# Early weights: two back steps alternate with the next weight's third and fourth front steps instead of its first and second

## The chip, the core and the metric

The kernel runs on one core of one Trainium2 chip. The metric is device time in microseconds; of several executions the median is given.

## The reference

Attention with exponential features, then two feed-forward layers, all in float32:

```python
def phi(x):                                  # for q and k, scaled
    proj = np.einsum('bhsd,md->bhsm', x, omega)
    sq = np.sum(x * x, axis=-1, keepdims=True) / 2.0
    h = proj - sq
    h = h - np.max(h, axis=-1, keepdims=True)
    return np.exp(h) / np.sqrt(m)
kv = np.einsum('bhsm,bhsd->bhmd', k_p, v)
num = np.einsum('bhsm,bhmd->bhsd', q_p, kv)
den = np.einsum('bhsm,bhm->bhs', q_p, z)[..., None] + 1e-06
...
xn = x / rms * rms_g
silu = g * (1.0 / (1.0 + np.exp(-g)))        # g = xn @ w_gate, val = xn @ w_val
x = (silu * val) @ w_out                     # first layer, d_ff 1536
g = h * np.cos(h)                            # h = x @ w_in
out = g @ w_out                              # second layer, d_ff 2048
```

There are 4 batches, 8 heads, 576 positions per batch (2304 tokens, 18 tiles of 128), head dimension 64, 128 features, model width 512.

## The kernel before

The work is one hand-written stream for each engine. First come 24 attention slots. Each slot projects one tile of 128 tokens (k tiles, with the first q tiles among them): TensorE multiplies by omega into two PSUM banks (`kp_ps` or `qp_ps`, L426), VectorE takes the maximum of each head (`kmx`, `qmx`, L435), ScalarE the exponential, head by head (`ke`, `qe`, eight a tile, L437). One slot later TensorE adds the k tile into its batch's sums (`kv_ps`, L587). When a batch is full, VectorE copies its two sums out (L598), which frees the banks for the next batch. A q tile goes through seven more steps, each in a later slot: transposes (`eT`, copied out half by VectorE, L454, and half by ScalarE, L452), the numerators (`num_ps`, L464) and quotients (L474 to L476), the square sum on ScalarE (`sq`, `ms`, L483), the root on GpSimd (L487, L488), the norm on VectorE (L492), a transpose (`xT_ps`, L502) and its split into high and low parts (`xhl`, L514, L516). Four banks are taken in turn by the projections and by `xT_ps`, so a projection waits until the exponentials of the tile that had the bank are done.

Then come FFN steps n = 0, 1, ...: products of a token block with a gate and a value weight (L831), their gating, and the output product (L884). The last q tiles go on beside them.

Beside all this the weights are made. They come as 64-bit floats: `raw` is a tile of pairs of 32-bit words, loaded by a DMA, and each weight must become a float32 (`f`) and then a pair of reduced-precision parts (`w`, high and low), so that three TensorE passes give nearly full precision. The class `Weights` holds this as generators whose steps are interleaved with the slots. The first 12 weights, c = 0 to 11, are the early ones (`self.fused`): they are made entirely in the attention slots and the first FFN steps. An early weight has six front steps (`front`, L186 to L211):

1. VectorE shifts `W` into `f` (L190);
2. only for a weight without signs in `W` (c = 2, 5, 8, 11): VectorE puts in the sign (L193);
3. VectorE masks the exponent into `raw` (L195);
4. ScalarE makes the next weight's `W` out of its `raw` (`exponent(c + 1)`, L182 or L184), so this waits for that raw weight's DMA;
5. VectorE multiplies the low word in (L204);
6. GpSimd adds both into `f` (L209).

and two back steps (`early_back`, `split`): ScalarE casts `f` to the high part of `w` (L214), behind which the load of raw weight c + 3 is issued on ScalarE's queue (L170); GpSimd subtracts for the low part (L217). `run` alternates the front steps of weight c with the back steps of weight c - 1, and every `tick` of a slot takes so many steps of `run`:

```python
for s in range(SLOTS):
    ...
    if s:
        wts.tick(5 if s < 6 else 1 if s < 14 else 4 if s + 1 < SLOTS else 0)
```

In the first FFN steps it is four steps for each half. Each engine takes its instructions strictly in the order in which the steps emit them; what stands behind a waiting instruction waits with it. Three raw tiles and three `f` tiles are held at a time, and one `W`.

Of the kernel before, what the change touches and what calls it, by code (L numbers as in the profile page):

```python
# [56 lines left out]
def attention_then_ffn(ctx: ExitStack, tc: tile.TileContext, qT, kT, v, omT, wc1, rms_g, wc2, out, B, H, S, D):  # L57
# [69 lines left out]
    class Weights:  # L127
# [186 lines left out]
        def run(self):  # L314

            self.exponent(0)
            yield
            for c in range(self.fused + 1):
                both = [self.front(c)] if c < self.fused else []
                if c > 0:  # L320
                    both.append(self.early_back(c - 1))
                while both:
                    for g in list(both):
                        if next(g, DONE) is DONE:
                            both.remove(g)
                        else:
                            yield
# [1102 lines left out]
```

## Time and profile before

| what | value |
|---|---|
| median of 3 runs | 966.22 us (966.13 to 969.75) |
| the profiled execution, its own time | 965.95 us |
| its span, from the first to the last instruction | 964.2 us |
| TensorE (PE) matmul / weight loads (PEld) | 951.0 us (99%) / 894.6 us (93%) |
| VectorE (DVE) / ScalarE (ACT) / GpSimd (POOL) | 710.2 us (74%) / 537.1 us (56%) / 415.5 us (43%) |
| ScalarE's casts of w (L214), 88 in all | 50.5 us, 580 ns each; 32.2 us of idle time before them |
| GpSimd's adds of f (L209), 68 in all | 94.3 us, 1387 ns each |
| granted clock of TensorE | 1.00 |

A profile's times count from the start of the span. The attention slots and the first FFN steps, in which the early weights are made, take about the first 130 us. Idle time is named with what ended it. Matmuls are pipelined, and their ends are modelled.

### The profile page before, as it was taken

Reading aid. Unit: us, or ns where it says so; the run is one execution under the profiler, and the core shown is the slowest. Engines: PE = TensorE matmul, PEld = TensorE weight load, DVE = VectorE, ACT = ScalarE, POOL = GpSimd, SP = SyncE. Lnnn points to the kernel's source line nnn. Section 1 sums busy time; section 2 is a strip of 40 time slices with the busy share of each in tenths; the row PEclk is TensorE's granted clock in tenths of the full one; section 3 lists DMA queues with packets and bytes.
Section 4 is the critical chain, followed back from the end, with each engine's and each line's share of the span. In section 5 each row is a group of like instructions: output and inputs, shape, how many; then the busy total and the mean of one; then the engine's idle time right before and its main releaser. Section 6 shows DMA issues by size and latency. Waiting matters only on the chain. (4 is left out here: it accounts for less than half of the span.)

```text
span 964.2 us, 16225 instructions
## 1 busy us (share of the span) xinstructions
PE 951.0 (99%) x5761; PEld 894.6 (93%) x5761; DVE 710.2 (74%) x1163; ACT 537.1 (56%) x1155; POOL 415.5 (43%) x377
## 2 busy tenths in 40 slices
PE   9999999999999999999999999999999999999998
PEld 8998999989999999999999998889889889889997
DVE  5786677778863686577685758996799777785766
ACT  7787776775543524355443545575655565464443
POOL 2133366657944867275764663320244220130000
PEclk9999999999999999999999999999999999999999
DMA  8565187778697898856989794967622768307554
GB/s 311 159 179 186 56 279 277 253 267 261 220 329 289 331 331 290 302 154 196 391 281 370 263 356 142 352 226 262 207 88 85 265 199 293 120 23 264 203 219 166
DMA packets 96082, 227.65 MB, mean 236 GB/s; under 512 B 9728, under 2 KB 45184, under 8 KB 96000
## 3 DMA queue, kind: packets, MB, share of 16 engines
q1 hardware_dynamic: 94704, 222.34, 67.0%
q10 hardware_dynamic: 1296, 4.26, 1.3%
q8 instruction: 46, 0.75, 0.3%
q14 instruction: 36, 0.29, 0.1%
HBM read 156.04 MB, written 70.52 MB: 235 GB/s over the span
## 5 line engine op out<-in xcount | busy, mean ns | idle before, releaser
L1251 PE MATMUL o_ps<-w,o 128*128 128x512 f32 x864 | 225.7, 393 | 0.7 <-DVE o L1054 0.7
L209 POOL TENSOR_TENSOR f<-f,raw 128x512 f32<-128x512 f32 x68 | 94.3, 1387 | 234.9 <-DVE raw L204 205.1
L1251 PEld LDWEIGHTS o_ps<-w,o 128*128 128x128 f32 x864 | 159.6, 188 | 25.0 <-DVE o L1054 1.1
L217 POOL TENSOR_TENSOR w<-b,w 128x512 fp32r<-128x512 f32 x88 | 115.3, 1316 | 136.7 <-ACT w L214 127.0
L831 PE MATMUL gv_ps<-xhl,w 128*128 128x384 f32 x576 | 108.0, 335 | 1.6 <-DVE gv L870 1.1
L831 PEld LDWEIGHTS gv_ps<-xhl,w 128*128 128x128 f32 x576 | 100.6, 188 | 2.2 <-DVE gv L870 1.4
L1150 PE MATMUL y<-t,w 128*128 128x384 f32 x576 | 102.1, 334 | 0.3 <-POOL w L217 0.3
L1150 PEld LDWEIGHTS y<-t,w 128*128 128x128 f32 x576 | 100.0, 188 | 0.6 <-POOL w L217 0.6
L1051 ACT CAST o<-turns 128x384 fp32r<-128x384 f32 x96 | 47.5, 513 | 95.0 <-DVE turns L1232 95.0
L1043 PE MATMUL Xh<-T,w 128*128 128x384 f32 x432 | 88.6, 340 | 1.7 <-ACT h L1196 1.7
L1043 PEld LDWEIGHTS Xh<-T,w 128*128 128x128 f32 x432 | 78.0, 188 | 9.2 <-ACT h L1196 4.0
L1043 PE MATMUL X<-T,w 128*128 128x384 f32 x432 | 80.9, 335 | 0.0
L1043 PEld LDWEIGHTS X<-T,w 128*128 128x128 f32 x432 | 75.3, 188 | 0.3 <-DVE r L1078 0.2
L214 ACT CAST w<-b 128x512 fp32r<-128x512 f32 x88 | 50.5, 580 | 32.2 <-DVE b L274 25.1
L1054 DVE TENSOR_TENSOR o<-turns,o 128x384 fp32r<-128x384 f32 x96 | 59.9, 640 | 8.2 <-ACT o L1051 8.1
L884 PE MATMUL y_ps<-t,w 128*128 128x384 f32 x288 | 60.7, 346 | 0.0
L1043 PE MATMUL Yh<-B,w 128*128 128x384 f32 x288 | 58.7, 338 | 0.0
L1199 DVE TENSOR_TENSOR h<-Yh,h 128x384 f32<-128x384 f32 x48 | 26.6, 553 | 42.4 <-PE Yh L1043 41.5
L1221 DVE SCALAR_TENSOR_TENSOR turns<-turns,r 128x768 f32<-128x768 int32 (+1 forms) x50 | 56.4, 1128 | 1.7
L1017 ACT ACTIVATE turns<-turns,half_pi 128x768 f32<-128x768 f32 (+1 forms) x50 | 45.7, 915 | 21.4 <-DVE turns L1221 21.3
L190 DVE TENSOR_SCALAR f<-W 128x512 int32<-128x512 int32 x68 | 44.8, 658 | 15.2 <-ACT W L182 6.5
L1043 PEld LDWEIGHTS Yh<-B,w 128*128 128x128 f32 x288 | 52.2, 188 | 3.8 <-ACT h L1196 0.2
(117 smaller groups left out, 1882.0 us busy)
## 6 DMA issues: line engine op xcount, KB each, us to landing
T<-T_dram SPq DMA_DIRECT2D x48, 768.0 KB, 7.0
raw<-wc SPq DMA_DIRECT2D x60, 512.0 KB, 4.9
B<-yh_dram SPq DMA_DIRECT2D x21, 768.0 KB, 5.4
kept<-f SPq DMA_DIRECT2D x56, 256.0 KB, 4.8
b<-kept SPq DMA_DIRECT2D x56, 256.0 KB, 4.9
B<-x_dram SPq DMA_DIRECT2D x15, 768.0 KB, 6.9
x_dram<-xhl SPq DMA_DIRECT2D x12, 768.0 KB, 5.8
s<-x_dram SPq DMA_DIRECT2D x24, 384.0 KB, 5.9
```

The lines of the kernel that those rows point to most:

```text
L209: nc.gpsimd.tensor_tensor(f32(f), f32(f), rest, op=ALU.add)
L214: nc.scalar.copy(t[:, 0, to], src)
L217: nc.gpsimd.tensor_tensor(t[:, 1, to], src, f32(t[:, 0, to]), op=ALU.subtract)
L831: nc.tensor.matmul(o, w[i], x[j], start=n == 0, stop=n == len(terms) - 1)
L884: nc.tensor.matmul(yacc[blk][e], w[:, i, e * P:(e + 1) * P], t[:, j], start=first and i + j == 0, stop=last and j == 1)
L1017: f(*args)
L1043: nc.tensor.matmul(o, w[:, i, c + kk * P:c + (kk + 1) * P], x[:, j, kk], start=begin and n == 0, stop=n == 5, skip_group_check=True)
L1051: nc.scalar.copy(t[:, 0], a)
L1054: engine.tensor_tensor(t[:, 1], a, f32(t[:, 0]), op=ALU.subtract)
L1150: nc.tensor.matmul(acc[e], w[:, i, e * P:(e + 1) * P], t[:, j], start=f == fs[0] and i + j == 0, stop=f == fs[-1] and j == 1)
L1221: nc.vector.scalar_tensor_tensor(r, a, -TWO_PI_LO, b, op0=ALU.mult, op1=ALU.add)
L1251: nc.tensor.matmul(oacc[blk][j], o[:, x, js], w[:, y], start=first and n == 0, stop=last and n == 2)
```

## The change

`run` lets the front generator of weight c take its first two steps alone; the back generator of weight c - 1 joins from the third round on (at once where there is no front left, for the last weight). A weight's eight steps were front 1, back 1, front 2, back 2, front 3, 4, 5, 6; they are front 1, 2, 3, back 1, front 4, back 2, front 5, 6.

```diff
             for c in range(self.fused + 1):
                 both = [self.front(c)] if c < self.fused else []
-                if c > 0:
-                    both.append(self.early_back(c - 1))
-                while both:
+                after = [self.early_back(c - 1)] if c > 0 else []
+                n = 0
+                while both or after:
+                    n += 1
+                    if n > 2 or not both:
+                        both += after
+                        after = []
                     for g in list(both):
                         if next(g, DONE) is DONE:
                             both.remove(g)
```

In the changed file the lines behind `run` are numbered four higher (L441 there is L437 here). The orders of TensorE, GpSimd and SP are the same but for these numbers. ScalarE's order moves in the early slots as follows. `ke3_0` are the exponentials of the first four heads of k tile 3; `w0`, `W3` and `raw3` belong to weights 0 and 3. Before:

```order
L437 ACTIVATE ke2_1_264<-kp_ps2_1_248,kmx2_1_265 128x128 x4
L214 CAST w0_283<-f0_239 128x512
L170 DMA raw3_285<-wc1 128x1024
L437 ACTIVATE ke3_0_302<-kp_ps3_0_292,kmx3_0_303 128x128 x4
L437 ACTIVATE ke3_1_309<-kp_ps3_1_293,kmx3_1_310 128x128 x4
L184 ACTIVATE W2_326<-raw2_201 128x512
L437 ACTIVATE ke4_0_343<-kp_ps4_0_333,kmx4_0_344 128x128 x4
L437 ACTIVATE ke4_1_350<-kp_ps4_1_334,kmx4_1_351 128x128 x4
L214 CAST w1_367<-f1_281 128x512
L170 DMA raw4_369<-wc1 128x1024
L437 ACTIVATE ke5_0_387<-kp_ps5_0_377,kmx5_0_388 128x128 x4
L437 ACTIVATE ke5_1_394<-kp_ps5_1_378,kmx5_1_395 128x128 x4
```

Changed, ScalarE at the same place:

```order
L441 ACTIVATE ke2_1_264<-kp_ps2_1_248,kmx2_1_265 128x128 x4
L441 ACTIVATE ke3_0_299<-kp_ps3_0_289,kmx3_0_300 128x128 x4
L441 ACTIVATE ke3_1_306<-kp_ps3_1_290,kmx3_1_307 128x128 x4
L214 CAST w0_321<-f0_239 128x512
L170 DMA raw3_323<-wc1 128x1024
L184 ACTIVATE W2_325<-raw2_201 128x512
L441 ACTIVATE ke4_0_343<-kp_ps4_0_333,kmx4_0_344 128x128 x4
L441 ACTIVATE ke4_1_350<-kp_ps4_1_334,kmx4_1_351 128x128 x4
L214 CAST w1_369<-f1_281 128x512
L170 DMA raw4_371<-wc1 128x1024
L182 ACTIVATE W3_373<-raw3_323 128x512
L441 ACTIVATE ke5_0_388<-kp_ps5_0_378,kmx5_0_389 128x128 x4
```

w0's cast and raw3's load moved behind the exponentials of k tile 3, and W3, which stood behind those of k tile 5, moved ahead of them. On VectorE the mask of raw1 (L195) moved ahead of the two maxima of k tile 3.

The second place is ScalarE around w4, in slots 15 and 16. Before, w4's cast stood between the exponentials of q tile 3 and k tile 12:

```order
L437 ACTIVATE qe3_1_862<-qp_ps3_1_846,qmx3_1_863 128x128 x4
L214 CAST w4_900<-f4_740 128x512
L170 DMA raw7_902<-wc1 128x1024
L437 ACTIVATE ke12_0_917<-kp_ps12_0_907,kmx12_0_918 128x128 x4
L437 ACTIVATE ke12_1_924<-kp_ps12_1_908,kmx12_1_925 128x128 x4
L514 CAST xhl0_0_774<-xT_ps1_931 128x2x128
L514 CAST xhl0_1_775<-xT_ps1_931 128x2x128
L483 ACTIVATE sq2_938,ms2_939<-x2_874 128x512
L452 COPY eT3_1_953<-eT_ps3_1_948 128x512
L182 ACTIVATE W6_958<-raw6_797 128x512
```

Changed, ScalarE at the same place:

```order
L441 ACTIVATE qe3_1_862<-qp_ps3_1_846,qmx3_1_863 128x128 x4
L441 ACTIVATE ke12_0_914<-kp_ps12_0_904,kmx12_0_915 128x128 x4
L441 ACTIVATE ke12_1_921<-kp_ps12_1_905,kmx12_1_922 128x128 x4
L518 CAST xhl0_0_774<-xT_ps1_928 128x2x128
L518 CAST xhl0_1_775<-xT_ps1_928 128x2x128
L487 ACTIVATE sq2_935,ms2_936<-x2_874 128x512
L456 COPY eT3_1_950<-eT_ps3_1_945 128x512
L214 CAST w4_953<-f4_740 128x512
L170 DMA raw7_955<-wc1 128x1024
L182 ACTIVATE W6_957<-raw6_836 128x512
```

w4's cast moved behind the square sum of q tile 2 (`ms2`) and the eT copy of q tile 3. GpSimd's order around it is the same before and after: w4's low part, then the two root steps of `ms2`, then the add of f5.

The third place is VectorE ahead of the maxima of k tile 17, the last k tile. Before:

```order
L204 SCALAR_TENSOR_TENSOR raw7_902<-raw7_902 128x512
L190 TENSOR_SCALAR f8_1220<-W8_1175 128x512
L435 TENSOR_REDUCE kmx17_0_1239<-kp_ps17_0_1228 128x4
L435 TENSOR_REDUCE kmx17_1_1246<-kp_ps17_1_1229 128x4
L193 SCALAR_TENSOR_TENSOR f8_1220<-W8_1175,f8_1220 128x512
L195 TENSOR_SCALAR raw8_1004<-f8_1220 128x512
```

Changed:

```order
L204 SCALAR_TENSOR_TENSOR raw7_955<-raw7_955 128x512
L190 TENSOR_SCALAR f8_1220<-W8_1174 128x512
L193 SCALAR_TENSOR_TENSOR f8_1220<-W8_1174,f8_1220 128x512
L439 TENSOR_REDUCE kmx17_0_1236<-kp_ps17_0_1225 128x4
L439 TENSOR_REDUCE kmx17_1_1243<-kp_ps17_1_1226 128x4
L195 TENSOR_SCALAR raw8_1062<-f8_1220 128x512
```

The sign step of f8 (L193) moved ahead of the two maxima. On ScalarE the cast of w7, which stood right ahead of the exponentials of k tile 17, moved behind them.

## Rows read from the trace of the kernel before

**Rows 1.** Windows, 10 to 90 us: us, busy time of each engine, clock, DMA.

```profile
10.00:90.00 80.00, 79.18 (x807) 72.95 (x804) 62.23 (x129) 66.74 (x220) 24.88 (x24) 1.00 0.65 211
```

**Rows 2.** Timeline of TensorE's weight loads: start, length, engine, line, what, count.

```profile
16.65 1.99 PEld L587 LDWEIGHTS kv_ps<-v,ke 128*128 128x128 f32 x16
...
29.39 1.86 PEld L587 LDWEIGHTS kv_ps<-v,ke 128*128 128x128 f32 x16
31.37 0.97 PEld L426 LDWEIGHTS qp_ps<-om,qraw 64*128 64x128 f32 x16
32.46 1.86 PEld L464 LDWEIGHTS num_ps<-kv,eT 128*128 128x128 f32 x16
```

**Rows 3.** Waits of ScalarE, 10 to 130 us: total us, times, longest.

```profile
ACT w L214 <- POOL f L209: 5.6, 6, 2.0
```

**Rows 4.** Timeline of ScalarE and, last two rows, VectorE in the early slots.

```profile
15.59 0.62 ACT L214 CAST w<-f 128x512 fp32r<-128x512 f32 x1 [0.50 <-POOL f L209]
15.65 0.37 ACTq L170 DMA_DIRECT2D raw<-wc  x1
16.12 2.18 ACT L437 ACTIVATE ke<-kp_ps,kmx 128x128 f32<-128x128 f32 x8
18.13 0.72 ACT L184 ACTIVATE W<-raw 128x512 f32<-128x512 f32 x1
...
21.22 2.29 ACT L437 ACTIVATE ke<-kp_ps,kmx 128x128 f32<-128x128 f32 x8
...
14.33 1.28 DVE L435 TENSOR_REDUCE kmx<-kp_ps 128x4 f32<-128x512 f32 x2
15.53 0.42 DVE L195 TENSOR_SCALAR raw<-f 128x512 int32<-128x512 int32 x1
```

**Rows 5.** Raw weights' landing: loads of ScalarE's queue (15 to 83 us), then all.

```profile
DMA to landing us min/median/max: 4.0/4.4/5.4
...
DMA to landing us min/median/max: 3.5/4.4/6.9
```

**Rows 6.** Timeline of TensorE's matmuls.

```profile
22.43 3.82 PE L587 MATMUL kv_ps<-v,ke 64*128 64x128 f32 x31
...
70.11 4.03 PE L587 MATMUL kv_ps<-v,ke 64*128 64x128 f32 x32
...
84.05 1.16 PE L426 MATMUL qp_ps<-om,qraw 64*128 64x128 f32 x14 [0.66 <-ACT ke L437]
```

**Rows 7.** Timeline of GpSimd, 59 to 66 us.

```profile
59.33 1.27 POOL L217 TENSOR_TENSOR w<-f,w 128x512 fp32r<-128x512 f32 x1 [0.73 <-ACT w L214]
62.71 0.19 POOL L487 TENSOR_SCALAR ms<-ms 128x1 f32<-128x1 f32 x1 [2.11 <-ACT sq L483]
62.98 0.55 POOL L488 TENSOR_TENSOR ms<-ms,minus_half 128x1 f32<-128x1 f32 x1
64.14 1.41 POOL L209 TENSOR_TENSOR f<-f,raw 128x512 f32<-128x512 f32 x1 [0.61 <-DVE raw L204]
```

**Rows 8.** Timeline of ScalarE, 62 to 85 us.

```profile
62.66 0.59 ACT L452 COPY eT<-eT_ps 128x512 f32<-128x512 f32 x1
...
82.33 0.62 ACT L214 CAST w<-f 128x512 fp32r<-128x512 f32 x1 [0.62 <-POOL f L209]
...
82.86 2.17 ACT L437 ACTIVATE ke<-kp_ps,kmx 128x128 f32<-128x128 f32 x8
```

**Rows 9.** Timeline of VectorE, 64 to 83 us.

```profile
64.32 1.77 DVE L492 SCALAR_TENSOR_TENSOR x<-x,ms,gain 128x512 f32<-128x512 f32 x1
...
68.69 0.75 DVE L598 COPY kv<-kv_ps 128x260 f32<-128x260 f32 x2
...
77.46 0.75 DVE L492 SCALAR_TENSOR_TENSOR x<-x,ms,gain 128x512 f32<-128x512 f32 x1
...
81.07 1.28 DVE L435 TENSOR_REDUCE kmx<-kp_ps 128x4 f32<-128x512 f32 x2
82.27 0.68 DVE L193 SCALAR_TENSOR_TENSOR f<-W,f 128x512 int32<-128x512 int32 x1
```

## The prediction

> **What bounds the kernel now.** I read the windows first. From 10 to 90 us, the stretch that holds most of the moved steps, TensorE shows 79.18 us of matmul in 80 us, all other engines less, at granted clock 1.00 [rows 1]. The reader should distrust that 79.18 a little, because a matmul that crawls counts as busy; so I read the weight loads next, whose share is 72.95 of 80. An undisturbed stretch prices their normal gaps: the loads that start at 29.39 and 31.37 are 1.86 and 0.97 us long, and the next group starts at 32.46, so 2.83 of 3.07 us are load and 7.8% is gap even where nobody waits [rows 2]. 7.8% of 80 is 6.25, the loads' idle time is 7.05: some 0.8 us of TensorE time is true waiting there. To it comes a group of loads that is stretched because ScalarE's exponentials feed it one head at a time: 1.99 us at 16.65 against 1.86 [rows 2], 0.13 us. So **all that this stage can give back is about 0.9 us**, 0.1% of the run, although ScalarE waits 5.6 us in six places for GpSimd in the very step that moves [rows 3]. Most of that wait lies beside TensorE's work.
>
> The profiled execution took 965.95 us (span 964.2); the median of the three runs is 966.22, 0.27 higher. I add the sum to either.
>
> **What the change does, part by part.** Work is neither added nor removed. Every early weight's two back steps (ScalarE's cast with the load of a raw weight behind it; GpSimd's low part) come two steps later, and the front steps between come one or two earlier. TensorE's, GpSimd's and SP's orders stay; ScalarE's and VectorE's change. After the attention stage the program is the same and TensorE stays full, so a shift of TensorE at 90 us should reach the end nearly whole.
>
> *The early slots.* Now the cast of w0 stands ahead of ke3's exponentials: it waits 0.50 us for f0's add and ke3 can start at 16.12 only [rows 4]. After, ke3 stands first, and VectorE's kmx3 gates it, which in turn has raw1's mask (0.42) put ahead of it: 14.33 + 0.42 + half of 1.28, some 15.4 [rows 4]. ke3 is 0.7 us earlier, and the loads at 16.65 are no longer fed one by one: **-0.13 us** (bounds 0 and -0.13).
>
> Against that stands raw3's load, a DMA on ScalarE's queue behind the cast: issued at 15.65 before, and some 17.7 after (ke3 from 15.4 takes 2.2). W3 moves the other way, ahead of ke5's exponentials. These loads take 4.0 to 5.4 us to land [rows 5], so raw3 is there at 21.7 to 23.1, while ScalarE, which began ke5 at 21.22 right behind w1's cast, is free for W3 near 21.6. W3 (0.72 by W2's row) and then ke5's 2.29 would end between 24.7 and 26.1, instead of 23.5 [rows 4]. TensorE uses ke5 in the second half of the accumulations that start at 22.43 and last 3.82, to 26.2 [rows 6]; at the undisturbed 1.98 for sixteen it starts there at 24.2 and needs the last exponential near 26.0. Cost **0**, bounds 0 and +0.3; were the load as slow as the slowest one of the start, 6.9 [rows 5], ke5 would end at 27.6 and TensorE lose 1.6. I take 0, as the median is 4.4.
>
> *The norm at 64 us.* This is where the change may hurt. GpSimd is in order: low part of w4, then the two ms2 steps, then f5's add. Now the low part is done at 60.6, ms2 runs from 62.71 to 63.53, and the add starts at 64.14 [rows 7]. After, w4's cast stands behind the eT copy that ends at 63.25, and lasts 0.62 [rows 8]: the low part runs from 63.9 to 65.2, ms2, stuck behind it, to 66.0 although its input was there at 62.7, and VectorE's norm, which ran at 64.32, starts 1.7 us later. The norm took 1.77 us with f5's add beside it and 0.75 alone [rows 9]; the add comes right behind ms2 again, so I take 1.77. From the norm VectorE is busy through kmx14 and the quotients to the copies of kv2 at 68.69 (0.75 for two) [rows 9], so these end near 70.8 and 71.1 instead of 69.1 and 69.4. TensorE's next accumulation needs the banks they clear; it started at 70.11 [rows 6] and would be due at 70.0 now. **+0.8 us**; bounds +0.1 (if the norm runs alone, 1.02 shorter) and +1.2 (if it needs both copies).
>
> The Trainium skill, "SBUF — State Buffer", section "SBUF: two separate sides", says that VectorE and GpSimd share one pair of ports as an exclusive lock: whoever starts first keeps it for its whole instruction, and a VectorE operation with two SBUF inputs waits it out. By that rule the norm would end 0.75 us after the add's 1.41, about 0.4 later than I took, the term would be +1.2 and the sum 0.4 higher. The row agrees in kind, not quite in size: 64.14 + 1.41 + 0.75 gives 66.30, and the norm ended at 66.09.
>
> *The wait at 84 us.* TensorE's one plain wait in the stage is 0.66 us on ScalarE before the row at 84.05 [rows 6]: qp5 needs a bank that the first four exponentials of ke17 clear, and these started at 82.86 because w7's cast (82.33, 0.62 us late on GpSimd) stood ahead [rows 8]. After, that cast is gone from there; but f8's sign step (0.68) now stands ahead of kmx17: 81.07 + 0.68 + half of 1.28 is 82.4 [rows 9], so ke17 can start 0.4 us earlier, if TensorE is on time. With TensorE 0.67 late by the terms above, what feeds kmx17 is as late, and ke17 starts at some 83.1: of the 0.67 us, 0.2 to 0.3 is left. **-0.4 us** (bounds 0 and -0.66).
>
> Costed at nothing: the casts of w8 to w10 move behind exponentials or copies in a stretch where ScalarE waits for VectorE and TensorE anyway; the casts and W steps that now stand together (w3 and W5, w5 and W7, w6 and W8) delay the exponentials behind them by up to one cast, 0.62 [rows 8], and TensorE uses these a group of matmuls later. If that cover were gone, each is worth its 0.62 once. The weights come two steps later and are first used when the FFN begins.
>
> **Sum**: -0.13 + 0 + 0.8 - 0.4 = +0.27 us: 966.2 for the profiled execution, **966.5** for the median. That is no change that a measurement of this kernel can tell (about 0.5%, 4.8 us).
>
> **Rivals.**
> 1. *Slower by the norm, with nothing given back.* The low part of w4 delays ms2, the norm and the copies at the upper bound of 1.2, and ke17 slides along so that the wait at 84 us stays: +1.2 - 0.13, 967.3. It decides once the norm starts over 0.6 us late, since the first copy ends 1.0 ahead of 70.11 and the rest is the bank's way to TensorE. For it: the fixed order and the busy VectorE. Against: 0.66 us of plain wait lies behind it.
> 2. *Slower by raw3.* The load lands in 6.9 us and W3 holds ke5: +1.6, and 0.1 of the rest, 967.9. Against: no load on ScalarE's queue took over 5.4.
> 3. *Faster.* The norm runs alone or beside nothing, and ke17 starts 0.4 us earlier: -0.13 - 0.4, 965.7, at most the 0.9 of the stage, 965.3. For it: the one long wait of the stage is touched.
> 4. *Much faster.* If every gap of the weight loads were headroom, 7.05 us could come back: 959.2. The gaps of the undisturbed stretch speak against it. The Trainium skill, "Perfetto Trace Analysis", section "Identifying the Most-Contended Engine", says to judge TensorE by its weight-load share rather than by matmul time; taken literally it reads the 72.95 this way.
> 5. *Slower by over 0.5%.* A load now has nine steps until its W, against twelve. The low part at 59.33 and the add at 64.14 are four steps apart, 4.8 us [rows 7], so nine are some 11 us. If loads took 12, each W would stall 1 us, seven times 7 us: 973. It decides at landings over 11 us; the rows say 4.0 to 5.4 [rows 5].
>
> **How the numbers follow.** Forecast (within 0.4 us of 966.5): 0.50. Rival 1: 0.20; 2: 0.08; 3: 0.17; 4: 0.02; 5: 0.03. The range runs from rival 3's floor, 965.3, to rival 2's 967.9, rounded up to 968.0; it leaves out rivals 4 and 5 and tails of the others. Faster by over 0.5%: rival 4, 0.02; slower: rival 5, 0.03; within: 0.95.
>
> **What would show it.** Right: ScalarE's wait for f's add falls from 5.6 us to under 1; ke3 starts near 15.4; ms2 runs behind w4's low part, near 65.2, and the norm near 66; the accumulation at 70.11 starts 0.5 to 0.8 later; the matmul at 84.05 is within 0.4 of its place. Wrong: TensorE over 1.5 us off its place at 90 us on either side, W3 waiting more than 1.5 us for raw3, or a difference that arises after 130 us, where the two programs are the same.

## The result, and the profile after

The changed kernel took **974.36 us** (median of 6 runs, 971.75 to 974.68), the kernel before, beside it, 967.25 (median of 6, 966.13 to 969.75): ratio **1.0066**, 95% interval 1.0049 to 1.0082. It is slower by 6 to 7 us (7.1 by the medians, 6.4 by the ratio). The forecast was 966.5, range 965.3 to 968.0, so it was wrong. The profiled execution took 974.35 us (span 972.6), the one of before 965.95: 8.40 us more.

The windows of the changed kernel: the first answers to [rows 1], the others are three short stretches that matter below. Columns as there; the clock stands ahead of the DMA share.

```profile
10.00:90.00 80.00, 76.20 (x746) 69.78 (x742) 61.87 (x116) 60.51 (x204) 23.19 (x23) 0.98 0.63 196
26.40:29.80 3.40, 3.40 (x19) 3.19 (x18) 1.32 (x3) 2.17 (x8) 0.92 (x1) 0.56 0.28 92
91.20:94.60 3.40, 3.40 (x36) 3.28 (x34) 2.71 (x7) 3.40 (x13) 1.28 (x1) 0.57 0.70 211
220.90:224.40 3.50, 3.50 (x13) 3.50 (x14) 3.46 (x6) 3.05 (x9) 3.34 (x3) 0.57 0.70 226
```

TensorE now has 76.20 us of matmul in the 80 where it had 79.18, and three stretches in which the granted clock is at its lower level, 1.2 GHz, nearly throughout (called half clock below). Before, it was 1.00 all along. What TensorE waits for between 9 and 135 us, the longest waits of the changed kernel:

```profile
PE kv_ps L591 <- DVE kv L602: 1.9, 2, 1.3
PE qp_ps L430 <- ACT ke L441: 1.3, 1, 1.3
PE kp_ps L430 <- ACT ke L441: 0.6, 1, 0.6
```

Of these, only the second existed before, with 0.66 [rows 6]. The first, 1.3 us of it at 24.97, is new. TensorE's timeline of the changed kernel, the rows that answer to [rows 6], each with the one that follows it:

```profile
24.97 5.62 PE L591 MATMUL kv_ps<-v,ke 64*128 64x128 f32 x32 [1.31 <-DVE kv L602]
30.52 0.72 PE L430 MATMUL kp_ps<-om,kraw 64*128 64x128 f32 x8
...
75.82 2.35 PE L591 MATMUL kv_ps<-v,ke 64*128 64x128 f32 x17 [0.58 <-DVE kv L602]
...
90.39 1.16 PE L430 MATMUL qp_ps<-om,qraw 64*128 64x128 f32 x14 [1.30 <-ACT ke L441]
91.48 3.56 PE L468 MATMUL num_ps<-kv,eT 128*64 128x128 f32 x32
```

The starts that were 22.43, 70.11 and 84.05 are 2.54, 5.71 and 6.34 us later (0.46 of it before 12 us, where nothing is moved yet), and behind the last of these rows, at 95 us, it is 7.9. After 130 us the difference goes up to 10 and back again, and ends at 8.4. So nearly all of it arises in the early stretch.

**Where VectorE lost it.** VectorE's timeline of the kernel before, the steps of f2 and what follows them; [rows 4] has the mask of raw1 at 15.53, 0.42 us:

```profile
18.88 0.45 DVE L190 TENSOR_SCALAR f<-W 128x512 int32<-128x512 int32 x1 [0.84 <-ACT W L184]
19.37 0.69 DVE L193 SCALAR_TENSOR_TENSOR f<-W,f 128x512 int32<-128x512 int32 x1
20.09 0.43 DVE L195 TENSOR_SCALAR raw<-f 128x512 int32<-128x512 int32 x1
20.44 1.28 DVE L435 TENSOR_REDUCE kmx<-kp_ps 128x4 f32<-128x512 f32 x2
21.64 0.75 DVE L598 COPY kv<-kv_ps 128x260 f32<-128x260 f32 x2
```

VectorE after, the same and the mask of raw1 with its maxima:

```profile
14.89 1.40 DVE L195 TENSOR_SCALAR raw<-f 128x512 int32<-128x512 int32 x1
16.20 1.28 DVE L439 TENSOR_REDUCE kmx<-kp_ps 128x4 f32<-128x512 f32 x2
...
20.20 1.03 DVE L190 TENSOR_SCALAR f<-W 128x512 int32<-128x512 int32 x1 [0.93 <-ACT W L184]
21.26 1.66 DVE L193 SCALAR_TENSOR_TENSOR f<-W,f 128x512 int32<-128x512 int32 x1
...
23.30 1.28 DVE L439 TENSOR_REDUCE kmx<-kp_ps 128x4 f32<-128x512 f32 x2
24.50 0.76 DVE L602 COPY kv<-kv_ps 128x260 f32<-128x260 f32 x2
...
70.98 1.76 DVE L496 SCALAR_TENSOR_TENSOR x<-x,ms,gain 128x512 f32<-128x512 f32 x1 [0.71 <-POOL ms L492]
...
86.90 1.67 DVE L193 SCALAR_TENSOR_TENSOR f<-W,f 128x512 int32<-128x512 int32 x1
88.49 1.28 DVE L439 TENSOR_REDUCE kmx<-kp_ps 128x4 f32<-128x512 f32 x2
```

And GpSimd after, at the same times:

```profile
14.61 1.39 POOL L209 TENSOR_TENSOR f<-f,raw 128x512 f32<-128x512 f32 x1 [11.77 <-DMA v<-v]
19.67 1.27 POOL L217 TENSOR_TENSOR w<-f,w 128x512 fp32r<-128x512 f32 x1 [3.68 <-ACT w L214]
20.91 1.46 POOL L209 TENSOR_TENSOR f<-f,raw 128x512 f32<-128x512 f32 x1
23.10 1.41 POOL L217 TENSOR_TENSOR w<-f,w 128x512 fp32r<-128x512 f32 x1 [0.73 <-ACT w L214]
...
70.92 1.28 POOL L209 TENSOR_TENSOR f<-f,raw 128x512 f32<-128x512 f32 x1
...
86.61 1.40 POOL L209 TENSOR_TENSOR f<-f,raw 128x512 f32<-128x512 f32 x1 [0.82 <-DVE raw L204]
```

Read the two together. The mask of raw1 ends at 16.29, 0.29 after the add beside it (16.00); the shift of f2 at 21.23, 0.29 after the low part of w0 (20.94); the sign steps at 22.92 and 88.57 end 0.55 and 0.56 after their adds (22.37, 88.01). So a step with one input ends 0.29 after GpSimd's instruction and a step with two 0.55, wherever it began: it waits for it, which experiment 5 tests. The mask takes 1.40 us where it took 0.42, the sign step 1.66 where it took 0.69. The maxima, which read PSUM, keep their 1.28 beside the low part at 23.10.

The Trainium skill, "SBUF — State Buffer", section "Who interferes with whom", says that a `tensor_scalar` can, where its operands allow it, use both of VectorE's port pairs, and that a step with two SBUF inputs needs the shared one beside a GpSimd instruction that reads SBUF; either is then blocked by the GpSimd instruction that started first, while on trn2 a `tensor_reduce` never contends. This trace agrees: 1.40, 1.66 and 1.28.

TensorE's accumulation at 24.97 needs the banks that the copies at 24.50 clear. Those stand behind the maxima, and these behind f2's steps. The sum on VectorE, in each trace's own time: f2 starts 1.32 later (0.46 of it before 12 us), its shift and sign take 0.58 and 0.97 longer, so the copies are 2.86 later.

### The profile page after: what moved, and what is told of

Its sections match the earlier page's. It is cut to its first block, busy times and chain, and to the rows that moved or that the text cites. A ratio compares the mean times of both kernels' runs of the same rounds, so it can differ in the third digit from the quotient of the medians.

```text
span 972.6 us, 16214 instructions
## 1 busy us (share of the span) xinstructions
PE 957.3 (98%) x5761; PEld 900.3 (93%) x5761; DVE 716.0 (74%) x1163; ACT 536.5 (55%) x1155; POOL 414.6 (43%) x377
```

## The experiments

The experiments write the order of `run` as a table of rounds, so that each part can be set alone (the code is shortened here; all lines behind it move by a few numbers). An "f" is the next front step, a "b" the next back step:

```python
for c in range(self.fused + 1):
    gens = {"f": self.front(c), "b": self.early_back(c - 1)}
    for step in plan(c):              # a step; "" is an empty one
        for g in step:
            next(gens[g])
        yield
OLD   = ["f", "b", "f", "b", "f", "f", "f", "f"]      # the kernel before
NEW   = ["f", "f", "f", "b", "f", "b", "f", "f"]      # the change
LATE  = ["f", "", "f", "b", "ff", "b", "f", "f"]      # back steps late, VectorE as before
EARLY = ["f", "fb", "f", "b", "", "f", "f", "f"]      # VectorE early, back steps as before
```

What each measured, in one table. The columns in the middle are worked out from the profiled executions: TensorE's matmuls are matched one by one with those of before, and the number is how much later they start near that time of before (us), less the difference at 12 us. Not all rows were measured side by side: the kernel before, run beside them, had 967.25 (the change), 966.23 (1 to 4), 966.70 (5 to 8) and 967.50 (9 and 10), so rows are compared by their ratios.

| run | at 22 | 33 | 61 | 79 | 84 | 90 | median | ratio to before, 95% |
|---|---|---|---|---|---|---|---|---|
| the change | 0.60 | 3.88 | 4.38 | 5.25 | 5.89 | 7.49 | 974.36 | 1.0066 (1.0049 to 1.0082) |
| 1 NEW for c > 2 only | 0.00 | 0.00 | 0.50 | 1.38 | 2.03 | 2.03 | 968.88 | 1.0032 (1.0020 to 1.0044) |
| 2 NEW for c <= 2 only | 0.63 | 5.53 | 5.53 | 5.53 | 5.54 | 5.54 | 972.68 | 1.0056 (1.0039 to 1.0072) |
| 3 LATE | -0.18 | 0.85 | 0.85 | 1.72 | 0.76 | 0.66 | 966.93 | 1.0005 (0.9995 to 1.0015) |
| 4 EARLY | 0.37 | 0.37 | 0.87 | 0.85 | 1.48 | 3.09 | 969.06 | 1.0021 (1.0012 to 1.0031) |
| 5 NEW, short adds | -0.15 | 0.36 | 0.35 | 0.33 | -0.01 | -0.01 | 967.25 | 1.0002 (0.9991 to 1.0013) |
| 6 NEW, filled wait | 0.61 | 2.32 | 2.82 | 3.70 | 4.34 | 4.32 | 971.48 | 1.0050 (1.0033 to 1.0067) |
| 7 OLD, w7 late | -0.02 | -0.02 | -0.03 | -0.02 | -0.98 | -1.08 | 965.46 | 0.9987 (0.9977 to 0.9996) |
| 8 OLD, sign x4 | -0.03 | 6.30 | 6.30 | 6.31 | 6.30 | 6.29 | 974.15 | 1.0075 (1.0058 to 1.0092) |
| 9 OLD, sign x4, filled | 0.00 | 3.18 | 3.18 | 3.18 | 3.19 | 3.17 | 971.28 | 1.0044 (1.0029 to 1.0060) |
| 10 LATE but w0, w1, w4 | 0.01 | 0.01 | 0.02 | 0.02 | -0.93 | -1.03 | 965.72 | 0.9986 (0.9977 to 0.9995) |

The theory after the result: VectorE's moved steps meet GpSimd's, are held up, and the clock falls behind the wait that follows ("ports"). The rival: the back steps that come later on ScalarE and GpSimd.

**1. Early weights as before.**

`plan` returns, for the rounds of weight c:

```python
                return OLD if c <= 2 else NEW
```

> The change's order for weights 3 to 11 only; the rounds of weights 1 and 2 go as before. Theory (ports): in the change the mask of raw1 and the two steps of f2 run beside GpSimd's adds, take about 1 us longer each, and hold up the maxima and the copies of kv0, after which TensorE's clock is granted at half for 3.4 us; that is 4.4 of the 7 us, so TensorE should start the accumulation of 24.97 near 22.5 again, with no half clock at 26 us, and the time be some 970. Rival (back steps): the later casts, loads and low parts cost it, at the norm and after; these stay, so 973 to 974.

Measured 968.88. The early stretch is as before (0.00 at 33 us), and 2.0 us are left: 0.50 at 61 us, where f5's sign step meets f4's add, 0.88 at the norm, 0.65 at 84 us, where f8's meets f7's. The wait of 1.30 us at 84 us is there as in the change, but in this execution no half clock followed it (2.03 at 84 us and at 90):

```profile
86.46 1.16 PE L433 MATMUL qp_ps<-om,qraw 64*128 64x128 f32 x14 [1.30 <-ACT ke L444]
```

**2. Early weights alone.**

```python
                return NEW if c <= 2 else OLD
```

> The complement: the change's order for weights 1 and 2 only, the rest as before. Theory (ports): the early wait and the half clock behind it stay, 967.3 + 4.4, so some 971.5, and the stretch from 60 to 95 us costs nothing more. Rival (back steps at the norm and later): 967 to 968.

Measured 972.68. The order of two weights carries most of the loss. Its wait of 1.3 us is the change's, but more than 6 us at half clock followed, where the change's execution had 3.4. The window of that stretch:

```profile
24.40:30.60 6.20, 6.20 (x30) 5.98 (x29) 2.06 (x4) 3.57 (x13) 2.66 (x2) 0.50 0.54 175
```

The eight executions of this run differ in the same way: the one with a mean granted clock of 1.00 took 968.13, the two with 0.998 970.41 and 971.98, the five with 0.996 took 972.21 to 973.94. Other differences of up to some 4 us stand beside this: the kernel before spreads that far with its clock at 0.997 to 1.00.

**3. The back steps alone.** `plan` is LATE for every c.

> One part of the change alone: casts, raw loads and low parts as late as in the change, VectorE's three steps (shift, sign, mask) where they were before. Theory (ports): the mask of raw1 takes about 0.42 us again and the sign step of f2 about 0.69, no early wait, no half clock; what is left is the norm's 0.5 to 0.8, so 967.5 to 968.5. Rival (back steps): 973 to 974.

Measured 966.93, no difference from before that the times can tell (the interval reaches up to 1.0015): without VectorE's moves the change costs next to nothing. But the expectation of f2's steps was wrong. VectorE, and behind it GpSimd, of this run:

```profile
17.94 1.03 DVE L190 TENSOR_SCALAR f<-W 128x512 int32<-128x512 int32 x1 [0.30 <-ACT W L184]
19.00 1.67 DVE L193 SCALAR_TENSOR_TENSOR f<-W,f 128x512 int32<-128x512 int32 x1
...
17.41 1.27 POOL L217 TENSOR_TENSOR w<-f,w 128x512 fp32r<-128x512 f32 x1 [2.25 <-ACT w L214]
18.64 1.48 POOL L209 TENSOR_TENSOR f<-f,raw 128x512 f32<-128x512 f32 x1
```

f2's steps are stretched here too, although VectorE's order is that of before. w0's late cast makes its low part late, GpSimd is in order, so f1's add is late too, and both fall on f2. That costs 1.03 us between 22 and 33 us, behind a wait of 0.64 us for the copies of kv0. The norm costs 0.87 more, and 0.96 come back at 84 us.

**4. VectorE's steps alone.** `plan` is EARLY for every c.

> The other part alone: VectorE's steps as early as in the change, casts, raw loads and low parts where they were before. Theory (ports): the masks and sign steps still meet GpSimd's adds, so the early wait, the half clock and the wait at 84 to 90 us come, without the norm's delay: 972 to 974. Rival (back steps): 967 to 968.

Measured 969.06, under half of the loss that the theory said. Here it is the other way round than in experiment 3:

```profile
14.35 1.41 DVE L195 TENSOR_SCALAR raw<-f 128x512 int32<-128x512 int32 x1
...
19.69 0.69 DVE L193 SCALAR_TENSOR_TENSOR f<-W,f 128x512 int32<-128x512 int32 x1
```

The mask of raw1 is stretched to 1.41 us, but w0's low part and f1's add come in time, f2's sign step takes 0.69, and there is no early wait (0.37 at 33 us). So the big early wait needs **both** parts of the change. At 33 us they cost 0.85 (experiment 3) and 0.37 alone, together 2.32 without the clock's part (experiment 6); no run divides the 1.1 us between further. The sign steps of f5 and f8 are stretched, which costs TensorE 0.50 and 0.63, and a half clock follows the wait at 84 us (3.09 at 90 us). "Ports" names the mechanism rightly, but not VectorE's order as its only cause.

**5. Without the collision.** Orders as in the change, the adds of the early weights cut to an eighth:

```diff
-            nc.gpsimd.tensor_tensor(f32(f), f32(f), rest, op=ALU.add)
+            some = slice(0, 64 if c < self.fused else 512)
+            nc.gpsimd.tensor_tensor(f32(f)[:, some], f32(f)[:, some], rest[:, some], op=ALU.add)
```

> The change's order, but GpSimd's adds of the 12 early weights cover 64 of 512 columns, so the low words of the other columns are left out of these weights. VectorE's steps and all orders are the same. Theory (ports): what stretches VectorE's steps is the add beside them, so the mask of raw1 takes 0.42 us and the sign steps of f2, f5 and f8 about 0.69, no wait over 0.5 us ahead of the accumulation at 24.97, no half clock, 967.5 to 969; f2's shift, which lies beside the low part of w0, stays near 1.03. Rival (the moved steps are long for another reason): 1.40 and 1.67 stay, 973 to 974.

Measured 967.25, as fast as before within the interval. VectorE of this run:

```profile
13.98 0.43 DVE L195 TENSOR_SCALAR raw<-f 128x512 int32<-128x512 int32 x1
...
18.32 1.03 DVE L190 TENSOR_SCALAR f<-W 128x512 int32<-128x512 int32 x1 [0.75 <-ACT W L184]
19.39 0.69 DVE L193 SCALAR_TENSOR_TENSOR f<-W,f 128x512 int32<-128x512 int32 x1
```

With short adds (0.43 and 0.50 us each) mask and sign step are back at 0.43 and 0.69, though they stand where the change puts them; the shift, beside the uncut low part of w0, stays at 1.03. That is the control within one run: only the steps whose neighbour was cut became short. A half clock came in this execution too, but not here (below, under what stays open). The norm costs nothing here either, which is the prediction's lower bound for a norm that runs alone.

**6. The wait without the clock's fall.** The change, with TensorE kept busy while it waits (a line elsewhere that keeps the idle matmuls' bank as `idle[0]` is left out here):

```diff
                 begin = (b, r) not in acc
+                if begin and (b, r) == (1, 0):
+                    for _ in range(8):
+                        nc.tensor.matmul(idle[0][:, 0:NB], zeros[:, 0:P], zeros, start=True, stop=True)
```

> The change with eight matmuls of zeros (384 columns, into the bank of the first idle ones, which nobody reads) ahead of the accumulation at 24.97, where TensorE waits 1.3 us for the copies of kv0. VectorE, ScalarE and GpSimd unchanged. Theory (the wait costs twice, once by itself and once by the clock that falls behind it): the accumulation starts where it did, within 0.3 us, but the clock stays at full from 26 to 30 us, TensorE is 2.6 us late at 33 us in place of 4.3, and the time is about 1.7 less, 972.7. Rival (the clock falls for another reason than this wait): half clock at 26 us as before, 974.4.

Measured 971.48. TensorE of this run:

```profile
23.52 1.48 PE L592 MATMUL idle_ps<-zeros 128*128 128x384 bf16 x8
24.92 4.03 PE L597 MATMUL kv_ps<-v,ke 64*128 64x128 f32 x32
28.88 1.16 PE L433 MATMUL kp_ps<-om,kraw 64*128 64x128 f32 x16
```

The accumulation starts at 24.92 (24.97 in the change) and takes 4.03 us in place of 5.62, at clock 1.00. The lateness at 33 us falls from 3.88 to 2.32: **1.56 us of the early loss are the clock**, the rest is the wait and what led to it. The other two half clocks did not come in this execution, though the 1.30 us wait at 84 us is there.

**8. VectorE's lateness alone.** The kernel before, with f2's sign step done four times:

```diff
-                nc.vector.scalar_tensor_tensor(f, w, SIGN, f, op0=ALU.bitwise_and, op1=ALU.bitwise_or)
+                for _ in range(4 if c == 2 else 1):
+                    nc.vector.scalar_tensor_tensor(f, w, SIGN, f, op0=ALU.bitwise_and, op1=ALU.bitwise_or)
```

> The kernel before, with f2's sign step done four times (the same result each time), so VectorE is some 2 us longer ahead of the maxima of k tile 5 and the copies of kv0, and nothing else moves. Theory (VectorE's lateness there is enough): the accumulation at 22.43 starts 1.7 to 2.1 us later, the clock falls to half behind that wait and takes another 1.7, so 3.4 to 4 us, 969.8 to 970.2. Rival (the wait alone, the clock of the change fell for another reason): 1.7 to 2.1, 968.

Measured 974.15: as slow as the change, with no order changed. VectorE, then TensorE, then the window:

```profile
19.50 3.94 DVE L194 SCALAR_TENSOR_TENSOR f<-W,f 128x512 int32<-128x512 int32 x4
...
25.50 7.03 PE L595 MATMUL kv_ps<-v,ke 64*128 64x128 f32 x32 [2.77 <-DVE kv L606]
...
25.60:32.40 6.80, 6.80 (x32) 6.40 (x32) 2.56 (x5) 4.52 (x15) 2.56 (x2) 0.53 0.38 119
```

Both sizes were short in the expectation: four steps took 3.94 us, not 2.8, as the last meets w1's low part, and more than 6 us at half clock followed, not 3.4.

**9. The same, filled.** Run 8 with 17 matmuls of zeros at the place of run 6.

> The kernel before with f2's sign step four times, as in the run in which TensorE waited 2.8 us and then ran 6.8 us at half clock, now with 17 matmuls of zeros ahead of that accumulation, some 2.9 us, to fill the wait. VectorE, ScalarE and GpSimd as in that run. Theory (the clock falls because TensorE stood idle): the accumulation starts within 0.4 us of 25.5, at full clock, TensorE is some 3.0 us late at 33 us in place of 6.45, and the time about 3.4 under that run's 974.2, 970 to 971. Rival (the clock's fall has nothing to do with the wait): half clock from 26 us, 974.

Measured 971.28. TensorE of this run:

```profile
22.53 2.94 PE L592 MATMUL idle_ps<-zeros 128*128 128x384 bf16 x17
25.40 4.03 PE L597 MATMUL kv_ps<-v,ke 64*128 64x128 f32 x32
```

The same lateness of VectorE costs 3.18 us in place of 6.30: the half clock is bound to TensorE's standing idle, and here it was half of the price. This is no luck of one profiled execution: the mean granted clock was 0.994 to 0.996 in all four executions of run 8 and 0.999 to 1.00 in all four of run 9, and 0.995 to 0.998 in the six of the change and 1.00 in all four of run 6.

**7 and 10. The part that pays.** Run 7 is OLD with LATE for c = 8 alone, which moves w7's cast and raw10's load behind the exponentials of k tile 17 and the xhl1 casts and nothing else; run 10 is LATE for c = 3, 4 and 6 to 11.

> The kernel before, with one thing moved: w7's cast and the load of raw10 stand behind the exponentials of k tile 17 and the xhl1 casts, VectorE's order untouched. Theory: the part of the forecast for the wait at 84 us was right where no VectorE step is moved, so the wait of 0.66 us goes and TensorE is 0.3 to 0.7 us early at 90 us; 965.6 to 966.0 against 966.2, less than the times can tell. Rival (kmx17 gates the exponentials anyway): wait stays over 0.4 us.

> VectorE's order untouched; casts, raw loads and low parts as late as in the change for w2, w3 and w5 to w10, those of w0, w1 and w4 where they were. So the early slots and the norm at 64 us stay as before. Theory: these late casts cost nothing, as the forecast had it, and w7's removes the wait at 84 us: TensorE 0.9 to 1.0 us early at 90 us, 965.3 to 965.7, like the run with w7 alone. Rival (the casts and W steps that now stand together delay exponentials): up to 0.6 us for each of three, so 966 to 967.5.

Measured 965.46 and 965.72; both intervals lie below 1. TensorE of run 7:

```profile
82.42 1.24 PE L433 MATMUL qp_ps<-om,qraw 64*128 64x128 f32 x16
83.59 0.66 PE L471 MATMUL num_ps<-kv,eT 128*64 128x128 f32 x8
```

From qp5's first matmul to the numerators it is 1.17 us. The kernel before, TensorE at the same place, with the row at 84.05 of [rows 6] between the two:

```profile
82.90 0.48 PE L426 MATMUL qp_ps<-om,qraw 64*128 64x128 f32 x2
...
85.13 1.10 PE L464 MATMUL num_ps<-kv,eT 128*64 128x128 f32 x16
```

There it is 2.23. The wait that is printed as 0.66 cost 1.06, because it is counted from the modelled end of the two matmuls ahead, not from the time at which the third could have started. Run 10 shows that the other late casts cost nothing. Between 7 and 10 the measurement sees no difference; each is faster than the kernel before, by 0.13% and 0.14%, and so faster than the change too.

## Why the prediction was wrong, by its own steps

The forecast's terms were -0.13 + 0 + 0.8 - 0.4 = +0.27 us. At 90 us the profiled execution had 3.88 in the early slots, 0.50 at f5's sign step, 0.87 at the norm, and 0.64 and 1.60 at the wait at 84 us: 7.49.

- **The early slots (-0.13, ke3 near 15.4; measured 3.88).** This step failed. It put "raw1's mask (0.42)" ahead of kmx3, with a duration from a row [rows 4] beside which GpSimd was all but idle: f0's add ended at 15.56, 0.03 us after the mask began. In its new place it runs beside that add and took 1.40; ke3 started at 16.91 (0.46 of this lateness is older than 12 us). Experiment 5 shows the mask back at 0.43 once the add is short.
- **Not costed: the cast of w0 and GpSimd's steps behind it.** This failed too, and was the larger miss. The prediction followed late casts to the exponentials, but for w4 alone to GpSimd's later instructions. At w0 the late low part pushed f1's add onto f2's sign step, ahead of the maxima and copies that TensorE waits for. Experiment 3 prices that part at 1.03 us; with the stretched mask ahead of it, it became a wait of 1.31. f5's sign step, moved ahead of maxima like f8's, stood in no term either.
- **The clock was no term at all.** The prediction read 1.00 in the windows and took it as given. The half clock behind the early wait cost 1.56 us (experiment 6), the one at 91 us 1.60: from 84 to 90 us the change's lateness grows from 5.89 to 7.49, that of experiment 1, with the same wait at full clock, not at all (2.03 to 2.03).

ScalarE's raw3 load and the other steps, point by point. Two rows of ScalarE's timeline, and one of its waits from 10 to 130 us, of the changed kernel:

```profile
16.91 0.88 ACT L441 ACTIVATE ke<-kp_ps,kmx 128x128 f32<-128x128 f32 x3 [1.39 <-DVE kmx L439]
...
23.00 0.71 ACT L182 ACTIVATE W<-raw 128x512 f32<-128x512 f32 x1
...
ACT w L214 <- POOL f L209: 0.6, 2, 0.5
```

- **raw3 (0, bounds 0 to +0.3) was right.** Rival 2 falls: the load, issued at 17.53, landed after 5.2 us, and W3 ran at 23.00 right behind w1's cast, with no wait for it. Rival 5 falls with it: the time came out near the one it gave, but not by its mechanism, so that was luck.
- **The norm (+0.8) was right**, in mechanism and size (by its own two numbers, 71.1 and 70.0, the upper bound should have read 1.1, not 1.2): w4's low part ran at 68.67, ms2 behind it, the norm took 1.76 beside f5's add, and TensorE lost 0.87 to 0.88 there in the change and in experiments 1 and 3. "Near 66" reads 70.98 only because all was 4.8 late by then.
- **The wait at 84 us (-0.4) had the right cause and the wrong duration.** Moving w7's cast away is worth 1.0 us (experiments 3, 7 and 10), more than the 0.66 that the row printed. But the prediction took 0.68 for f8's sign step from a row with GpSimd idle [rows 9]; beside f7's add it took 1.67, kmx17 came at 88.49, and the gain turned into 0.64 lost, with a half clock behind it.
- **ScalarE's wait for f's add falls under 1 us**: right, 5.6 to 0.6 us. It had been as free as the prediction said.
- **"All that this stage can give back is about 0.9 us"**: about right; experiments 7 and 10 got 1.0. Rival 4 falls with it. But the bound says nothing of what a change can cost.

One rule was in the text already: the lock between VectorE and GpSimd was used for the norm, but not for the two sign steps (f5, f8) that the change moved next to a GpSimd add. They have two SBUF inputs as the norm has, and each took about 1 us longer. For raw1's mask, with one input, the sentence that the prediction quoted was not enough; and w0's late low part and the clock would still have been missing.

What stays open: why behind the same wait of 1.30 us one execution has a half clock and another has none, and the third half clock, at 220.9. It follows TensorE's waits of 0.94 and 0.43 us, which the kernel before has nearly alike (0.90 and 0.42) at full clock, and experiment 5 had one at that place. Most of what it costs comes back at the next wait on VectorE. Nothing here tells why.

## What to carry to other kernels

When a VectorE step with two SBUF inputs, or a `tensor_scalar` from SBUF to SBUF, is moved, look at what GpSimd does at its new place, and take the duration from a row with the same neighbour. In a kernel whose engines run in order, a late instruction also moves everything behind it on its engine: follow it until it meets another engine's work. And a wait of TensorE of 1.3 us or more can cost up to twice, because the clock may fall behind it; where the wait can't be removed, cheap matmuls in it can give that part back, as they did in experiments 6 and 9 (1.56 and 3.12 us).

## What the runs showed of the hardware

- VectorE's shift and mask of a 128x512 int32 tile took 1.03 and 1.40 us beside a GpSimd instruction against 0.42 to 0.45 alone, and ended 0.29 us after it; the two-input sign step took 1.66 to 1.67 against 0.69 and ended 0.55 after it.
- After waits of 1.3 us, TensorE's granted clock was at its lower level for 3.4 us in the change and in experiment 4, for more than 6 us in experiment 2, and not at all in experiments 1 and 6 behind the same wait at 84 us; after 2.77 us (experiment 8), for more than 6 us. The same wait doesn't fix the price.
- The 32 matmuls of that accumulation took 4.03 us at 2.4 GHz throughout, 5.62 and 7.03 with the clock at 1.2 GHz for a part or nearly all of them.
